# A fused attention and MLP block: one ring of eight raw buffers in the projection, and the MLP's weights staged earlier

## The chip, the cores and the metric

The kernel runs on one core of one Trainium2 chip. The metric is device time in microseconds (us) of one execution, lower is better. Three runs of the kernel before took 1137.27, 1138.0 and 1139.82 us; their median is 1138.0 us.

## The reference

For 2048 tokens of width 448, a gate mixes an attention block of 16 heads (28 wide) and an MLP of inner width 1792. Everything is float32.

```python
qkv = (x @ wqkv) -> q, k, v            # 16 heads of 28
p   = softmax(q @ k.T * 28 ** -0.5)
a   = (p @ v, heads joined) @ wo
y   = layernorm(x)                     # no scale, eps 1e-5
h   = gelu(y @ w1 + b1)                # 448 -> 1792, tanh form
b   = h @ w2 + b2                      # 1792 -> 448
g   = sigmoid((x * gate_w).sum(-1))
out = g * a + (1 - g) * b
```

## The kernel before

**Split operands.** Nearly every float32 operand of a product is split in two: a high part (rounded by ScalarE, ACT, with an `AF.Copy` into the type float32r) and a low part (the raw value minus the high part, a `tensor_sub` on VectorE, DVE, or GpSimd, POOL). A product is then three matmuls on TensorE (PE): high by high, high by low, low by high. So a weight that comes from memory goes through four steps: a DMA into a raw buffer, issued by SyncE (SP), the high part on ACT, the low part on DVE or POOL, and the matmuls. Below, "splitting" a piece means its high and its low part.

**Three stages.** The tokens are worked in four chunks `c` of 512 (`CH`).

1. Projection of q, k, v (`qk_tile`, `v_tile`). For each chunk there are seven tiles `m` of 128 columns of q and k, 11 matmuls each (L179), and then four tiles of 128 tokens of v, 11 matmuls each (L195). A q/k tile is evicted from PSUM by ACT and DVE into one of three `hl` buffers (L181, L182) and stored to `qk` in memory (L183, 512 KB); a v tile goes through one of three `vt` buffers (L197) to `vs` (L199). PSUM has eight banks, and the tiles take them in turn (`next_ps`), so PE may run up to eight tiles ahead of the evictions. The chunk's input is four raw tiles of x (`load_x`, L165 to L170), which are loaded and split while the v tiles of the chunk before are issued. Beside this, chunks 1 and 2 load x a second time for the statistics of the layer norm (`bxr`, L209), and chunks 2 and 3 normalise the MLP's first chunk on POOL and ACT (`ln_apply`, L127 to L133). The raw buffers are two rings here: `wraw`, four buffers for weights, and `xraw`, four for x and the weights of v.
2. MLP (`mlp1`, `mlp2`). For each chunk, 14 tiles `f` of the first layer, 11 matmuls each (L512), into banks 0 and 1 in turn; ACT reads a tile twice (L515, L516: GELU into `hh` and `h`), POOL makes its low part `hl` (L517). Then the second layer for four tiles of 128 tokens, 42 matmuls each (L525, L526, L529). In chunk 0 the weights are still being staged: in each tile `f` the piece `w1[f+3]` and the piece `w2[f]` are fetched, and after `mlp1(c, f)` the pieces `w1[f+2]` and `w2[f-1]` are split (`split_w1`, `split_w2`). The raw buffers for this are four: `s0`, `s1` and the two halves of `lnr`.
3. Attention (`scores`, `pv_mm`), then the output projection.

**The row maxima.** The softmax needs each row's maximum, found from a first, coarse product of q and k: 1024 matmuls of 28 rows (L346), whose results DVE reduces (L326 one bank, L328 two banks). They are spread over the MLP and the attention by a `Filler`: each matmul of the MLP adds its cost to a counter, and when six are due, six row-maximum matmuls into banks 2 to 7 are put between two others. `MLP_MAX` of the 1040 steps (the matmuls and 16 transposes) fall into the MLP, the rest into the attention, three in each pass of its loop. Their keys are in `khr`, loaded in 16 DMAs of 28 rows by 512 (`load_khr`, L408).

**What sets the order.** PE's order is that of the code. In the MLP and the attention the other engines and the SP queue follow the code as well (`tc.manual_schedule`). In the projection a scheduler orders the other engines. All of SP's DMAs go through one queue in order: one that waits for a buffer holds back those behind it.

Of the kernel before, what the change touches and what calls it, by code (L numbers as in the profile page):

```python
# [7 lines left out]
F32 = mybir.dt.float32  # L8
F32R = mybir.dt.float32r
AF = mybir.ActivationFunctionType  # L10
# [30 lines left out]
def kernel(ctx: ExitStack, tc: tile.TileContext, xt, wqk, wv, wo, xk, w1, b1, w2, b2,  # L41
                          ident_d, sel_d, out):
    nc = tc.nc
# [14 lines left out]
    qk = dram.tile([2, 2 * D, S], F32, name="qk")  # L58
# [23 lines left out]
    w1h, w1l, w2h, w2l = {}, {}, {}, {}  # L82
# [10 lines left out]
    def fetch_w1(f):  # L93
        wraw[1, f] = staged()
        nc.sync.dma_start(wraw[1, f], w1[f].rearrange("p t x -> p (t x)"))

    def split_w1(f, lo):
        r = wraw.pop((1, f)).rearrange("p (t x) -> p t x", t=4)
        t = mw1.tile([P, 8, P], F32R, name=f"w1f{f}")
        w1h[f], w1l[f] = t[:, 0:4], t[:, 4:8]  # L100
        nc.scalar.activation(w1h[f], r, AF.Copy)
        lo.tensor_sub(w1l[f], r, w1h[f].bitcast(F32))  # L102

    def fetch_w2(f):
        wraw[2, f] = staged(D)
        nc.sync.dma_start(wraw[2, f], w2[f])

    def split_w2(f):
        r = wraw.pop((2, f))
        nc.scalar.activation(w2h[f], r, AF.Copy)  # L110
        nc.vector.tensor_sub(w2l[f], r, w2h[f].bitcast(F32))

    yh, yl = (my.tile([P, n, CH], F32R, name=f"y{n}") for n in (4, 3))
    lnr = my.tile([P, 2, CH], F32, name="lnr")
# [21 lines left out]
    with tc.tile_pool(name="qx", bufs=2) as qx, tc.tile_pool(name="qo", bufs=3) as qo, \  # L136
# [4 lines left out]
        def next_ps():  # L141
            nonlocal nps
            nps += 1
            return bank[:, nps % 8]

        def load_wqk(m):
            raw = qx.tile([P, 4, P], F32, name="wraw", bufs=4)
            nc.sync.dma_start(raw, wqk[m])
            wh[m] = qw.tile([P, 4, P], F32R, name=f"wh{m}")
            wl[m] = qw.tile([P, 4, P], F32R, name=f"wl{m}")  # L150
            nc.scalar.activation(wh[m], raw, AF.Copy)
            nc.gpsimd.tensor_sub(wl[m], raw, wh[m].bitcast(F32))

        wvh = qw.tile([P, 4, 450], F32R, name="wvh")
        wvl = qw.tile([P, 4, 450], F32R, name="wvl")
        vt = [qw.tile([P, H, 32], F32, name=f"vt{i}") for i in range(3)]

        xh, xl = {}, {}

        def load_x(c, t):  # L160
            if t == 0:
                xh[c] = qx.tile([P, 4, CH], F32R, name="xh")
                xl[c] = qx.tile([P, 3, CH], F32R, name="xl")
            raw = qx.tile([P, CH], F32, name="xraw", bufs=4)
            nc.sync.dma_start(raw, xt[t, :, c * CH:(c + 1) * CH])  # L165
            nc.scalar.activation(xh[c][:, t], raw, AF.Copy)
            if t < 3:
                nc.vector.tensor_sub(xl[c][:, t], raw, xh[c][:, t].bitcast(F32))
            else:
                nc.vector.tensor_sub(xh[c][64:128, t], raw[64:128], xh[c][64:128, t].bitcast(F32))  # L170

        def qk_tile(c, m):
            ps = next_ps()
# [58 lines left out]

        load_wqk(0)
        for t in range(4):
            load_x(0, t)
        load_wqk(1)
        for c in range(NC):
            for m in range(NM):
                if c == 0:
                    if m + 2 < NM:  # L240
                        load_wqk(m + 2)
                    if m == 1:
                        for v in vt:
                            nc.gpsimd.memset(v[:, :, DH:DH + 1], 1.0)
                            nc.gpsimd.memset(v[:, :, DH + 1:32], 0.0)
                    if m == 4:
                        for t in range(4):
                            raw = qx.tile([P, 450], F32, name="xraw", bufs=4)
                            nc.sync.dma_start(raw, wv[:, t])
                            nc.scalar.activation(wvh[:, t], raw, AF.Copy)  # L250
                            nc.gpsimd.tensor_sub(wvl[:, t], raw, wvh[:, t].bitcast(F32))
                qk_tile(c, m)
                if c == 1 and m >= 2 or c == 2 and m < 3:
                    ln_stats(m - 2 if c == 1 else m + 5)
                if c == 1 or c == 2 and m == 0:
# [17 lines left out]
                    ln_rows(TPC, NT)  # L273
                if c == 3 and m == 4:
                    ln_turn(TPC, NT)
                if c == 3 and m in (1, 2, 4):
                    if m == 2:
                        stages += [lnr[:, 0], lnr[:, 1]]
                    fetch_w1(m // 2)
                if c == 3 and m in (4, 5):  # L280
                    split_w1(m - 4, nc.vector)
            for i in range(TPC):
                if c + 1 < NC:
                    load_x(c + 1, i)
                v_tile(c * TPC + i)

    class RowMax:

# [112 lines left out]

    khi = dict.fromkeys(range(MLP_G + 1), khr)

    def load_khr(g, k):

        for j in range(4):
            r = D + (4 * g + j) * DH
            nc.sync.dma_start(khr[32 * j:32 * j + DH, k * CH:(k + 1) * CH].bitcast(F32), qk[0, r:r + DH, k * CH:(k + 1) * CH])  # L408

    def load_khi(g):  # L410
        if g == MLP_G:
# [107 lines left out]
    def mlp2(c, i):  # L519

        sl = slice(i * P, (i + 1) * P)
        last = c * TPC + i == NT - 1
        a = bank[:, 7 if last else i % 2, :D]
        for f in range(NF):
            nc.tensor.matmul(a, hh[f][:, sl], w2h[f], start=(f == 0), stop=False)  # L525
            nc.tensor.matmul(a, hh[f][:, sl], w2l[f], start=False, stop=False)  # L526
            if not last:
                filler.run(2 * W2)
            nc.tensor.matmul(a, hl[f][:, sl], w2h[f], start=False, stop=(f == NF - 1))  # L529
            if not last:  # L530
                filler.run(W2)
            elif f == NF // 3:
# [6 lines left out]
    with tc.manual_schedule(engines={E.SP, E.Pool, E.Activation, E.DVE}):  # L539
        for c in range(NC):  # L540
            for f in range(NF):
                if c == 0:
                    if f + 3 < NF:
                        fetch_w1(f + 3)
                    fetch_w2(f)
                    if f == 0:
                        filler.max = RowMax()
                    if f < 4:
                        load_khr(0, f)
                    if f == FS:  # L550
                        filler.spread(nc.sync, MLP_MAX, 11 * W1 * (0.8 * (NF - FS) + 3 * NF) + 3 * W2 * NF * (NT - 1))
                mlp1(c, f)
                if c == 0:
                    if f + 2 < NF:
                        split_w1(f + 2, nc.vector if f < FS else nc.gpsimd)
                    if f > 0:
                        split_w2(f - 1)
            if c == 0:
                split_w2(NF - 1)
                stages[2:] = []  # L560
            if c == NC - 1:
                m0.close()
# [265 lines left out]
```

## Time and profile before

| what | value |
|---|---|
| median of three runs | 1138.0 us |
| time of the profiled execution | 1136.69 us |
| its span | 1134.9 us |
| PE busy | 1114.4 us, 98% of the span |
| DVE / ACT / POOL busy | 739.6 / 634.6 / 323.8 us |
| mean granted TensorE clock | 0.995 |
| moved by DMA | 84.35 MB |

In this execution the projection runs from 0 to 121 us, the MLP to 474 us and the attention to the end. The "granted clock" is the share of full speed at which TensorE was run. A row of the timeline shows start, duration, engine, line, operation and, in brackets, how long the engine sat idle before and what ended that. Matmul durations overlap, so the distance from one start to the next is what a matmul costs.

### The profile page before, as it was taken

To read this page: it belongs to the slowest core of one execution; us is meant where nothing else is said; L and a number is where in the kernel's file an instruction comes from. 1 tells how busy PE (TensorE), PEld (TensorE's weight loads), DVE (VectorE), ACT (ScalarE), POOL (GpSimd) and SP (SyncE) were. 2 spreads that over 40 slices of the span, in tenths; PEclk is the share of its full clock that TensorE was granted. 3 is DMA by queue.
4 is the path that set the end of the run, shared out by engine and by line. 5 is a ranking of instruction groups with operands and counts; after the bars stand their busy time and mean duration, and the time that the engine had idled before them with its cause. 6 is when DMAs were issued, how large, how long until landed. Compare 5 with 4: busy or idle time off the path is not lost.

```text
span 1134.9 us, 19822 instructions
## 1 busy us (share of the span) xinstructions
PE 1114.4 (98%) x8136; PEld 675.8 (60%) x8136; DVE 739.6 (65%) x1037; ACT 634.6 (56%) x668; POOL 323.8 (29%) x349
## 2 busy tenths in 40 slices
PE   7999999999999999999999999999999999999998
PEld 6878767767767767744444444444444444464556
DVE  3542498888888888576666766667666667646103
ACT  5333660241231132188787877878877788746563
POOL 4005373334333331013113211320223125425050
PEclk9999999999999999999999999999999999999999
DMA  8986642011110105063000220002111003011101
GB/s 264 298 263 230 214 129 72 26 46 35 48 56 25 36 9 129 25 154 99 23 25 19 60 65 24 22 28 51 35 48 36 22 15 93 12 50 51 59 27 50
DMA packets 53519, 84.35 MB, mean 74 GB/s; under 512 B 8676, under 2 KB 28660, under 8 KB 52628
## 3 DMA queue, kind: packets, MB, share of 16 engines
q1 hardware_dynamic: 49236, 76.96, 22.2%
q0 software_dynamic: 4192, 6.12, 2.3%
q8 instruction: 64, 1.05, 0.4%
q14 instruction: 27, 0.22, 0.1%
HBM read 56.40 MB, written 26.49 MB: 73 GB/s over the span
## 4 chain that ended last, share of the span: by engine, by line
PE 90%; DMA 3%; DVE 2%; POOL 2%; issue 1%; ACT 1%; SPq 1%; POOLq 0%; ACTq 0%
PE bank L713 22%; PE bank L466 20%; PE bank L346 15%; PE bank L512 11%; PE bank L179 5%; PE bank L529 4%; PE bank L525 4%; PE bank L526 4%; DMA xraw<-in_xt 2%; PE bank L195 2%; PE bank L618 1%; PE bank L619 1%; PE bank L620 1%; POOL w1f L102 1%; DVE mx L328 1%
## 5 line engine op out<-in xcount | busy, mean ns | idle before, releaser
L471 ACT ACTIVATE pt<-bank 128x1536 f32<-128x1536 f32 (+1 forms) x408 | 482.3, 1234 | 154.0 <-PE bank L466 154.0
L326 DVE TENSOR_REDUCE mx<-bank 128x1 f32<-128x512 f32 x624 | 413.3, 687 | 175.9 <-PE bank L346 162.3
L713 PE MATMUL bank<-pt,vg 128*32 128x512 f32 x2038 | 262.5, 605 | 0.0
L328 DVE TENSOR_REDUCE mx<-bank 128x2 f32<-128x1024 f32 x200 | 235.3, 1218 | 32.3 <-PE bank L346 32.3
L346 PE MATMUL bank<-khi,qd 28*128 28x512 f32 x512 | 241.8, 479 | 1.3 <-DVE mx L326 1.3
L346 PEld LDWEIGHTS bank<-khi,qd 28*128 28x128 f32 x512 | 92.3, 181 | 148.9 <-DVE mx L326 105.4
L466 PE MATMUL bank<-qh,klo 28*128 28x512 f32 x1024 | 177.4, 393 | 0.0
L466 PE MATMUL bank<-qh,khi 29*128 29x512 f32 x768 | 160.0, 481 | 0.0
L512 PE MATMUL bank<-y,w1f 128*128 128x512 f32 x616 | 154.3, 399 | 3.8 <-POOL w1f L102 2.7
L512 PEld LDWEIGHTS bank<-y,w1f 128*128 128x128 f32 x616 | 111.9, 188 | 41.8 <-issue 12.6
L466 PE MATMUL bank<-ql,khi 28*128 28x512 f32 x768 | 132.2, 390 | 0.0
L517 POOL TENSOR_TENSOR hl<-h,hh 128x512 fp32r<-128x512 f32 x56 | 72.4, 1293 | 135.9 <-ACT h L516 93.8
L713 PEld LDWEIGHTS bank<-pt,vg 128*32 128x32 f32 x2038 | 45.6, 108 | 84.1 <-issue 83.5
L515 ACT ACTIVATE hh<-bank,b1s 128x512 fp32r<-128x512 f32 x56 | 38.6, 689 | 99.3 <-PE bank L512 99.2
L466 PEld LDWEIGHTS bank<-qh,klo 28*128 28x128 f32 x1024 | 89.3, 185 | 4.1
L525 PE MATMUL bank<-w2h,hh 128*128 128x448 f32 x224 | 84.0, 375 | 1.8 <-DVE mx L326 1.8
L634 POOL DMA_DIRECT2D lt<-ob x15 | 10.9, 724 | 261.1 <-DVE ob L633 261.1
L529 PE MATMUL bank<-w2h,hl 128*128 128x448 f32 x224 | 85.3, 381 | 0.0
L535 ACT ACTIVATE h<-bank 128x448 f32<-128x448 f32 x16 | 8.7, 546 | 135.4 <-PE bank L529 101.0
L466 PEld LDWEIGHTS bank<-qh,khi 29*128 29x128 f32 x768 | 62.3, 182 | 36.5 <-ACT pt L471 32.2
L526 PE MATMUL bank<-w2l,hh 128*128 128x448 f32 x224 | 82.5, 368 | 0.0
L346 PE MATMUL bank<-khr,qd 28*128 28x512 f32 x512 | 81.0, 466 | 0.2
(112 smaller groups left out, 1241.6 us busy)
## 6 DMA issues: line engine op xcount, KB each, us to landing
qk<-hl SPq DMA_DIRECT2D x28, 512.0 KB
xraw<-in_xt SPq DMA_DIRECT2D x16, 256.0 KB
vs<-vt SPq DMA_DIRECT2D x16, 256.0 KB
s<-in_xt SPq DMA_DIRECT2D x16, 256.0 KB
rc<-rls POOLq DMA_DIRECT2D x60, 64.0 KB, 2.3
bxr<-in_xk SPq DMA_DIRECT2D x8, 448.0 KB
gbs<-h SPq DMA_DIRECT2D x16, 224.0 KB
klo<-qk SPq DMA_DIRECT2D x16, 224.0 KB
```

The costliest lines, as they stand in the source:

```text
L179: nc.tensor.matmul(ps, a, b, start=(i == 0), stop=(i == len(ops) - 1))
L326: nc.vector.reduce_max(self.mx[:, c0:c0 + 1], bank[:, b0], axis=AX)
L328: nc.vector.reduce_max(self.mx[:, c0:c1 + 1:c1 - c0], bank[:, b0:b1 + 1], axis=AX)
L346: nc.tensor.matmul(bank[:, b], self.qds[self.n][r, i * P:(i + 1) * P], khi[self.n // NC][r, k * 512:(k + 1) * 512], start=True, stop=True)
L466: nc.tensor.matmul(bank[:, u % U], a[r, k * P:(k + 1) * P], b[r], start=(i == 0), stop=(i == 2))
L471: nc.scalar.activation(t, bank[:, b:b + len(units)], AF.Exp, scale=SCALE)
L512: nc.tensor.matmul(ps, a, b, start=(i == 0), stop=(i == len(ops) - 1))
L517: nc.gpsimd.tensor_sub(hl[f], h, hh[f].bitcast(F32))
L525: nc.tensor.matmul(a, hh[f][:, sl], w2h[f], start=(f == 0), stop=False)
L526: nc.tensor.matmul(a, hh[f][:, sl], w2l[f], start=False, stop=False)
L529: nc.tensor.matmul(a, hl[f][:, sl], w2h[f], start=False, stop=(f == NF - 1))
L713: nc.tensor.matmul(pv[32 * j:32 * j + 32, :], vg[n // NC][:, k, 32 * j:32 * j + 32], probs.pop(4 * step + j), start=(k == 0), stop=(k == N ...
```

## The change

It has five parts.

1. In the projection the two rings of four raw buffers become one ring of eight (`raw`), which q/k weights, v weights and x share. The v weights are asked for in tile 3 of chunk 0 and not in tile 4. Fetch and split of x are parted: chunk `c+1`'s four raw tiles are fetched at tiles 3 to 6 of chunk `c`, and split after tiles 5 and 6 and ahead of the first two v tiles; before, both stood ahead of the four v tiles.
2. Seven of the 14 pieces of `w1` (before: the splits of two) are fetched into that ring and split during chunk 3 of the projection, their low parts on DVE and POOL in turn.
3. The other seven pieces of `w1` and the 14 of `w2` pass through the four staging buffers in the order `order`, one and a half per tile `f`. A piece's high part is made in one tile and its low part in the tile that follows, ahead of that tile's matmuls. All seven of these low parts of `w1` are POOL's.
4. The row maxima's first keys come in four DMAs of 28 rows by 2048, not 16 of 28 by 512.
5. `MLP_MAX` is 482, not 476. The last but one token tile (`NT - 2`) takes no row-maximum step in its last four `f`, and the attention spreads the rest over two passes fewer.

```diff
-MLP_MAX = 476
+MLP_MAX = 482
...
+        def raw():
+            return qx.tile([P, CH], F32, name="raw", bufs=8)
...
-        def load_x(c, t):
+        def fetch_x(c, t):
+            xraw[c, t] = raw()
+            nc.sync.dma_start(xraw[c, t], xt[t, :, c * CH:(c + 1) * CH])
+
+        def split_x(c, t):
...
+                if c + 1 < NC and m >= 3:
+                    fetch_x(c + 1, m - 3)
                 qk_tile(c, m)
+                if c + 1 < NC and m >= 5:
+                    split_x(c + 1, m - 5)
...
-                if c == 3 and m in (1, 2, 4):
-                    if m == 2:
-                        stages += [lnr[:, 0], lnr[:, 1]]
-                    fetch_w1(m // 2)
-                if c == 3 and m in (4, 5):
-                    split_w1(m - 4, nc.vector)
+                if c == 3:
+                    fetch_w1(m, raw())
+                    if m >= 2:
+                        high_w1(m - 2)
+                        low_w1(m - 2, nc.vector if m % 2 else nc.gpsimd)
             for i in range(TPC):
-                if c + 1 < NC:
-                    load_x(c + 1, i)
+                if c + 1 < NC and i < 2:
+                    split_x(c + 1, i + 2)
                 v_tile(c * TPC + i)
+                if c == 3 and i < 2:
+                    high_w1(i + 5)
+                    low_w1(i + 5, nc.vector if i else nc.gpsimd)
...
+            rows = not last and (c * TPC + i < NT - 2 or f < 10)
...
+        order = [x for i in range(7) for x in (NF + 7 + i, i)] + list(range(7, NF))
...
+            return order[max(0, 3 * (f - 1) // 2 - 1):max(0, 3 * f // 2 - 1)]
...
-                    if f + 3 < NF:
-                        fetch_w1(f + 3)
-                    fetch_w2(f)
                     if f == 0:
+                        stages += [lnr[:, 0], lnr[:, 1]]
                         filler.max = RowMax()
-                    if f < 4:
-                        load_khr(0, f)
+                    for k in stage(f - 1):
+                        low(k)
+                    for k in order[3 * f // 2:3 * (f + 1) // 2]:
+                        fetch_w2(k) if k < NF else fetch_w1(k - NF, staged())
+                    for k in stage(f):
+                        high(k)
+                    if f == 1:
+                        load_khr(0)
...
-    filler.spread(nc.gpsimd, NG * NC * 65, ((NG * NC - 2) * NT + LQ - 1) * 4 // U)
+    filler.spread(nc.gpsimd, NG * NC * 65, ((NG * NC - 2) * NT + LQ - 1) * 4 // U - 2)
```

The SP queue in the projection, from the second half of chunk 1's q/k tiles to its v tiles, before (`xraw<-in_xt` is a raw tile of x for chunk 2, `qk<-hl` a store of a q/k tile, `bxr<-in_xk` x for the statistics, `vs<-vt` a store of a v tile):

```order
L183 DMA qk<-hl 128x2x512 x2
L165 DMA xraw<-in_xt 128x512
L183 DMA qk<-hl 128x2x512
L165 DMA xraw<-in_xt 128x512
L183 DMA qk<-hl 128x2x512
L199 DMA vs<-vt_113 128x512
L165 DMA xraw<-in_xt 128x512
```

and the same stretch of the queue now:

```order
L168 DMA raw<-in_xt 128x512
L218 DMA bxr<-in_xk 128x2x448
L192 DMA qk<-hl 128x2x512 x2
L168 DMA raw<-in_xt 128x512
L192 DMA qk<-hl 128x2x512
L218 DMA bxr<-in_xk 128x2x448
L192 DMA qk<-hl 128x2x512
L208 DMA vs<-vt_113 128x512
```

The last raw tile of x for chunk 2 stood behind the stores of tiles 5 and 6 and the first v store; now it stands ahead of these three.

On ACT, at the start of the MLP (`hh` and `h` are the two GELU reads of a tile `f`, `w1f` and `w2h` the high parts), before:

```order
L515 ACT_TABLE_LOAD
L515 ACTIVATE hh_1063<-bank,b1s 128x512
L516 ACTIVATE h<-bank,b1s 128x512
L101 ACTIVATE w1f_1094<-lnr 128x512
L515 ACTIVATE hh_1061<-bank,b1s 128x512
L516 ACTIVATE h<-bank,b1s 128x512
L101 ACTIVATE w1f_1118<-s_96 128x512
L110 ACTIVATE w2h_1009<-s_97 128x448
```

and now:

```order
L532 ACT_TABLE_LOAD
L532 ACTIVATE hh_1089<-bank,b1s 128x512
L533 ACTIVATE h<-bank,b1s 128x512
L532 ACTIVATE hh_1087<-bank,b1s 128x512
L533 ACTIVATE h<-bank,b1s 128x512
L100 ACTIVATE w1f_1137<-s_97 128x512
L110 ACTIVATE w2h_1035<-lnr 128x448
```

Before, the first `w1f` here is the piece that tile 2 multiplies with; now it is that of tile 7.

On PE, the last two groups of row-maximum steps in the MLP, before (`w2h`, `w2l` with `hh`, `hl` are the second layer; the row behind the `x2` opens the last token tile):

```order
L346 MATMUL bank<-khr,qd 128x512 x6
L529 MATMUL bank<-w2h_1033,hl_1040 128x448
L525 MATMUL bank<-w2h_1035,hh_1037 128x448
L526 MATMUL bank<-w2l_1036,hh_1037 128x448
L529 MATMUL bank<-w2h_1035,hl_1038 128x448
L346 MATMUL bank<-khr,qd 128x512 x2
L525 MATMUL bank<-w2h_1009,hh_1063 128x448
```

and now (the row behind the `x2` is the eleventh `f` of the same token tile, so 12 matmuls stand between it and the last token tile):

```order
L362 MATMUL bank<-khr,qd 128x512 x6
L547 MATMUL bank<-w2h_1051,hl_1074 128x448
L542 MATMUL bank<-w2h_1053,hh_1071 128x448
L543 MATMUL bank<-w2l_1054,hh_1071 128x448
L547 MATMUL bank<-w2h_1053,hl_1072 128x448
L362 MATMUL bank<-khr,qd 128x512 x2
L542 MATMUL bank<-w2h_1055,hh_1069 128x448
```

More of the change, by code (lines that the diff above doesn't have):

```diff
@@ L106, in fetch_w2, with high_w2, low_w2 @@
         nc.sync.dma_start(wraw[2, f], w2[f])
[L108 to L111, printed above, removed]
+    def high_w2(f):
+        nc.scalar.activation(w2h[f], wraw[2, f], AF.Copy)
+    def low_w2(f):
+        nc.vector.tensor_sub(w2l[f], wraw.pop((2, f)), w2h[f].bitcast(F32))
     yh, yl = (my.tile([P, n, CH], F32R, name=f"y{n}") for n in (4, 3))
@@ L539, with high, low, stage @@
     with tc.manual_schedule(engines={E.SP, E.Pool, E.Activation, E.DVE}):
+        order = [x for i in range(7) for x in (NF + 7 + i, i)] + list(range(7, NF))
+        def high(k):
+            high_w2(k) if k < NF else high_w1(k - NF)
+        def low(k):
+            low_w2(k) if k < NF else low_w1(k - NF, nc.gpsimd)
+        def stage(f):
+            return order[max(0, 3 * (f - 1) // 2 - 1):max(0, 3 * f // 2 - 1)]
         for c in range(NC):
```

69 lines of the change are left out of this document (35 added, 34 removed).

## The prediction

> **What bounds the kernel now.** I read the page first: who is busy, and where the slices of the span are not full.
>
> ```profile
> PE 1114.4 (98%) x8136; PEld 675.8 (60%) x8136; DVE 739.6 (65%) x1037; ACT 634.6 (56%) x668; POOL 323.8 (29%) x349
> ```
>
> TensorE is the bound; what can be gained without taking matmuls away is its idle time and the matmuls that run at a lower clock. Next, who PE waits for (us in total, times, longest):
>
> ```profile
> PE bank L179 <- ACT xh L166: 6.1, 1, 6.1
> PE bank L512 <- POOL w1f L102: 2.7, 5, 1.0
> PE bank L179 <- DVE xh L170: 2.4, 1, 2.4
> PE bank L525 <- DVE mx L326: 1.8, 1, 1.8
> PE bank L512 <- DVE w1f L102: 1.0, 2, 0.7
> ```
>
> The first is the start of the program, whose first five DMAs the change leaves as they are. The other four are the change's aims. Then stretches around the two longest of them (busy time of each engine, and behind POOL the granted clock, the DMA share and GB/s):
>
> ```profile
> 64.20:67.10 2.90, 0.47 (x2) 0.03 (x1) 0.71 (x2) 1.40 (x3) 0.00 (x0) 1.00 0.85 309
> 68.60:72.00 3.40, 3.40 (x9) 2.67 (x8) 1.45 (x6) 0.79 (x2) 0.00 (x0) 0.51 0.82 108
> 471.30:474.00 2.70, 2.70 (x9) 2.34 (x8) 0.00 (x0) 0.00 (x0) 0.00 (x0) 0.50 0.00 0
> ```
>
> A wait costs twice: shortly after PE resumes, the clock is at half for some 3 us (0.51 and 0.50).
>
> **The change part by part.** All sums are against the profiled execution: span 1134.9, time 1136.7, which is 1.3 us under the median of the three runs and 0.6 under the lowest.
>
> *x for chunk 2.* PE's timeline, with the first two matmuls of the chunk and the first at full clock again:
>
> ```profile
> 62.05 0.40 PE L179 MATMUL bank<-xh,wh 128*128 128x512 f32 x1
> 62.28 0.40 PE L179 MATMUL bank<-xl,wh 128*128 128x512 f32 x1
> ...
> 72.00 0.40 PE L179 MATMUL bank<-xh,wh 128*128 128x512 f32 x1
> ```
>
> Between 62.05 and 72.00 run two tiles: 22 matmuls at 0.23 us (62.05 to 62.28) and two short transposes make 5.2 us; 9.95 passed. So 4.7 us are lost, wait and half clock together. The fourth raw tile of x was issued late, behind stores:
>
> ```profile
> 56.72 0.36 SPq L183 DMA_DIRECT2D qk<-hl  x1
> 58.09 0.39 SPq L183 DMA_DIRECT2D qk<-hl  x1
> 59.55 0.33 SPq L199 DMA_DIRECT2D vs<-vt  x1
> 59.94 1.17 SPq L165 DMA_DIRECT2D xraw<-in_xt  x1
> ```
>
> It now stands ahead of two stores of 512 KB and one of 256, which is 1.28 MB or about 4 us at the 309 GB/s above. It was needed 2.4 us sooner than it came, so the wait goes: **-4.7**.
>
> *The first weights.* Chunk 0's and chunk 1's first layers (x154 matmuls; the next number but one is first to last start):
>
> ```profile
> L512 PE MATMUL bank<-y,w1f x154: 387/389/504, 121.0 to 167.4; 128*128 128x512 f32 x154
> L512 PE MATMUL bank<-y,w1f x154: 387/389/501, 211.3 to 256.0; 128*128 128x512 f32 x154
> 215.84 0.73 PE L346 MATMUL bank<-khr,qd 28*128 28x512 f32 x6
> 216.50 3.49 PE L512 MATMUL bank<-y,w1f 128*128 128x512 f32 x14
> 219.92 0.73 PE L346 MATMUL bank<-khr,qd 28*128 28x512 f32 x6
> ```
>
> One group of six row-maximum steps and 14 matmuls take 4.08 us (215.84 to 219.92); 14 at 0.23 are 3.2, so a group costs about 0.86. Chunk 1 has 12 groups in its 44.7 us, chunk 0 has six: without waits it would take 44.7 - 5.2 = 39.5. It takes 46.4; the two estimates of a matmul, 0.23 and slightly less, leave an excess of 6.3 to 6.9, say 6.6 us. The reason is that each piece of `w1` is ready just in time, behind POOL's work on the tile before:
>
> ```profile
> 154.01 0.73 PE L512 MATMUL bank<-y,w1f 128*128 128x512 f32 x2 [0.99 <-POOL w1f L102]
> 151.44 1.30 POOL L517 TENSOR_TENSOR hl<-h,hh 128x512 fp32r<-128x512 f32 x1 [1.87 <-ACT h L516]
> 152.69 1.27 POOL L102 TENSOR_TENSOR w1f<-lnr,w1f 128x512 fp32r<-128x512 f32 x1
> ```
>
> Now pieces 0 to 6 lie ready when the MLP starts, and piece `f` from 7 on is complete two to four tiles ahead. What is late next is ACT: a high part that waits for its DMA holds back the GELU reads behind it, and with two banks PE stands two tiles later. The closest is the piece for tile 9: its buffer is freed by POOL behind `hl` of tile 2 (1.30 + 1.27 us), the DMA takes about 3.1 (99.47 to 102.53 below), and ACT wants it one tile later. I leave 0.7 us for that (0 to 3.3, half of the excess): **-5.9**.
>
> *A new wait at tile 2.* Tile 2 needs bank 0 back from the first GELU reads. ACT before:
>
> ```profile
> 99.47 0.33 SPq L95 DMA_DIRECT2D s<-in_w  x1
> 102.53 0.63 ACT L101 ACTIVATE w1f<-s 128x512 fp32r<-128x512 f32 x1 [3.59 <-DMA s<-in_w]
> 103.06 0.62 ACT L129 ACTIVATE y<-s 128x512 fp32r<-128x512 f32 x1
> 110.19 0.60 ACT L181 ACTIVATE hl<-bank 128x512 fp32r<-128x512 f32 x1 [3.80 <-DMA qk<-hl]
> 122.52 0.55 ACT L197 ACTIVATE vt<-bank 128x448 f32<-128x448 f32 x1 [3.05 <-DMA vs<-vt]
> 124.96 0.68 ACT L516 ACTIVATE h<-bank,b1s 128x512 f32<-128x512 f32 x1
> ```
>
> In chunk 3 ACT does not follow PE: its evictions stand behind the layer norm's `y` (103.06), then wait for stores to free `hl` and `vt`, and the reads of tile 0 end at 125.6. PE will be 4.7 us earlier, so it starts the MLP at 116.3 and wants bank 0 two tiles (5.1 us) later, at 121.4. If ACT's chain doesn't move, PE waits 4.2 us; if it moves by as much as PE, nothing. The chain begins at the load of `lnr`, behind the x tiles and stores of chunk 2, which leave when the v tiles of chunk 1 are evicted, no longer stuck behind the late x: I take half of 4.7, so a wait of 1.9. The half clock followed idle gaps of 1.8 and 2.4 us, and not one of 0.99; 3.4 and 2.7 us at half speed (the stretches above) cost 1.7 and 1.3, on average 1.5, of which I take half. **+2.6** (0 to 5.7). By the Trainium skill (TensorE: Matmul & The Clock Gate, Part 1: The HAM clock gate) the clock falls after an idle window of about 3.4 us. By that rule this term is 1.9 alone; the trace differs, with half clock after 2.4 and 1.8 us.
>
> *The end of the staging.* Four low parts of `w2` instead of two now stand on DVE right ahead of the row maxima of the second layer's first groups:
>
> ```profile
> 170.39 0.61 DVE L111 TENSOR_TENSOR w2l<-lnr,w2h 128x448 fp32r<-128x448 f32 x1
> 174.39 1.09 PE L346 MATMUL bank<-khr,qd 28*128 28x512 f32 x6
> ```
>
> Two more are 1.2 us, and the group at 174.39 already waits for DVE (1.09 against the 0.73 at 215.84). **+1.0** (0 to 1.5).
>
> *The end of the MLP.*
>
> ```profile
> 467.46 0.50 PE L346 MATMUL bank<-khr,qd 28*128 28x512 f32 x2
> 469.79 0.47 PE L525 MATMUL bank<-w2h,hh 128*128 128x448 f32 x1 [1.82 <-DVE mx L326]
> 470.10 0.36 PE L526 MATMUL bank<-w2l,hh 128*128 128x448 f32 x1
> 470.30 0.37 PE L529 MATMUL bank<-w2h,hl 128*128 128x448 f32 x1
> ...
> 471.32 0.58 PE L526 MATMUL bank<-w2l,hh 128*128 128x448 f32 x1
> 471.69 0.58 PE L529 MATMUL bank<-w2h,hl 128*128 128x448 f32 x1
> ```
>
> The last token tile uses bank 7, which DVE still reduces: 2.3 us from 467.46 to 469.79, of which 0.3 would pass anyway. Now 12 matmuls of 0.20 us (470.10 to 470.30), 2.4 us, stand in between, so the reductions are done in time. From 471.3 a matmul takes 0.37; eight of them at 0.17 over are 1.3. **-3.3** (-2.5 if 0.8 of the wait stays).
>
> *Six more row-maximum steps in the MLP* are one more group, **+0.9**. In the attention six fewer, a group of six takes 0.73 us by itself (215.84), so at most 0.7, and I take **-0.2**, since other matmuls run beside them
> *Taken at nothing*: the fetch of the last q/k weights and of the v weights in chunk 0 (PE has no wait there after the start; a low part of POOL that came late would cost up to its 1.3 us), and the keys in four DMAs. The first of these waits for a store of chunk 3, and the v stores behind it could be held back; the stores in front of them are later than that anyway. If not, it adds to the wait at tile 2, inside its bounds.
>
> **Sum**: -4.7 - 5.9 + 2.6 + 1.0 - 3.3 + 0.9 - 0.2 = -9.6, so 1127.1 against 1136.7. The timed runs lie 0.6 to 3.1 over the profiled one; adding 0.9, I forecast 1128.0.
>
> **The rivals.**
>
> *All covers hold*: ACT's chain moves as far as PE, no wait at tile 2 or behind the staging, none in it: 2.6 + 1.0 + 0.7 less, 1123.7. For it: the chain's first link is the stores that the late x held up. Against it: the stores' waits (3.80, 3.05) are the memory's pace, and more weights are loaded there.
>
> *What chunk 2 gains, tile 2 gives back*: ACT's chain stays, PE waits 4.2 us and pays a full half-clock phase, 3.1 more than the forecast: 1131.1; with half of the staging excess kept, 1133.7. For it: POOL's layer norm stands on a load of its own, and has a low part of `w1` more in front of it.
>
> *x still comes late*: the earlier fetch is eaten by a full memory (the DMA share was 0.85 there), and PE's wait stays; then the wait at tile 2 is gone too, 1128.0 + 4.7 - 2.6 = 1130.1.
>
> *The staging loop becomes the bound* (slower): 21 pieces pass through four buffers, 5.25 rounds each. A round is a DMA (3.1), a high part (0.63) in ACT's turn, POOL's `hl` and the low part (2.6), one tile later by rule. Without waits the stage takes 46.4 - 6.6 = 39.8 us, which allows 7.6 us a round. At 10 us it takes 52.5, which is 6.1 over the old stage in place of 5.9 under it: 1128.0 + 12.0 = 1140.0. From there on the change is slower. Against it: before, 26 pieces went through four buffers in 46.4 us, 7.1 us a round, and that with each piece in demand at once. For it: high and low part now stand a tile apart.
>
> **How the numbers follow.** 0.2% of 1138.0 is 2.3 us, about what a measurement of this kernel tells from no change: faster is below 1135.7, slower above 1140.3. Chances: the forecast 0.50, all covers 0.15, tile 2 gives back 0.15, x still late 0.06, the staging loop 0.14, of which 0.09 above 1140.3 and 0.05 between. That makes 0.86 faster, 0.05 the same, 0.09 slower. The range goes from 1122.5, just under the case of all covers, to 1135.5, over the two rivals in the middle with the unknown ends of the other terms; it leaves out the staging loop and a little below.
>
> **What would show it.** Right: no wait for `xh` near 62 us and the granted clock at 1.00 there; the MLP's first matmul near 116 us; the first layer of chunk 0 no longer than 43 us; no wait for `w1f`; at the MLP's end no wait for `mx` and no half clock. The new wait would stand at tile 2, ended by ACT `h`. Wrong: a wait over 5 us at tile 2, evictions that stop PE in chunk 3, or tiles of chunk 0 that stand behind ACT all along.

## The result, and the profile after

The changed kernel takes 1139.83 us (median of 14 runs), the kernel before 1138.49 us (14 runs, 1136.72 to 1139.82). Twelve runs of the changed kernel lie at 1138.3 to 1140.7 us, the two others at 1133.67 and 1130.73. The ratio on record is 1.0002 (the quotient of the two medians is 1.0012), with a 95% interval of 0.9987 to 1.0017: no difference that can be told, where 1128.0 us was forecast with a range up to 1135.5. The profiled execution of the changed kernel takes 1140.1 us with a span of 1138.32, which is 3.4 us over the span before (1134.89). The stages lie so (us; a stage ends where PE starts the next one's first matmul):

| stage | before | after | difference | forecast |
|---|---|---|---|---|
| projection | 120.99 | 117.25 | -3.7 | -4.7 |
| MLP chunk 0, first layer | 46.7 | 49.0 | +2.3 | -3.3 |
| MLP chunk 0, second layer | 43.6 | 47.8 | +4.2 | +1.9 |
| MLP, chunk 1 to chunk 3's first layer | 223.3 | 223.5 | +0.2 | 0 |
| chunk 3, second layer | 39.8 | 37.1 | -2.7 | -3.3 |
| attention, to PE's end | 656.8 | 654.2 | -2.6 | -0.2 |
| from PE's end to the end of the span | 3.7 | 9.4 | +5.7 | 0 |

The windows of the changed kernel at the places of the prediction (busy time of PE, PEld, DVE, ACT and POOL, the granted clock, the DMA share, GB/s), the first two and the sixth being the old waits:

```profile
64.00:67.00 3.00, 3.00 (x16) 2.34 (x15) 1.41 (x6) 0.50 (x1) 0.00 (x0) 1.00 0.95 277
68.60:72.00 3.40, 3.40 (x17) 2.78 (x16) 2.67 (x10) 1.31 (x3) 0.00 (x0) 1.00 1.00 296
122.35:128.59 6.24, 0.08 (x1) 0.00 (x1) 0.16 (x1) 3.14 (x5) 0.00 (x0) 0.71 0.97 342
128.60:132.70 4.10, 4.10 (x11) 3.25 (x12) 0.85 (x1) 2.08 (x4) 2.52 (x2) 0.61 0.50 108
176.10:179.50 3.40, 3.40 (x11) 2.99 (x11) 1.82 (x2) 0.00 (x0) 2.55 (x2) 0.51 0.01 5
471.60:474.40 2.80, 2.80 (x15) 2.61 (x14) 0.00 (x0) 0.55 (x1) 0.00 (x0) 1.00 0.22 82
1132.00:1137.50 5.50, 0.00 (x0) 0.00 (x0) 0.00 (x0) 0.00 (x0) 0.00 (x0) 0.50 0.00 0
```

The waits aimed at are gone, with full clock at 64 to 72 us and at 472. In their place stand a hole of 6.2 us at tile 2 with a half-clock stretch behind it, another half-clock stretch at 176, and 5.5 us at the very end in which no engine is busy and no DMA moves. Who PE waits for says the same of the first:

```profile
PE bank L529 <- ACT h L533: 6.4, 2, 6.2
PE bank L188 <- ACT xh L175: 5.8, 1, 5.8
PE bank L362 <- DVE mx L344: 1.5, 4, 0.6
```

(L188, L529, L362 are now the matmuls of the q/k tiles, of the MLP's first layer and of the row maxima.) The hole at the end is in no list of waits, since nothing computes after it. It shows in the line at which the program ends: counts, then minimum, median and maximum in ns. Before and after:

```profile
L823 POOLq DRAIN  x3: 40/102/1412, 1128.9 to 1134.6; - x3
```

```profile
L856 POOLq DRAIN  x3: 40/102/10967, 1126.6 to 1138.1; - x3
```

POOL's last subtraction begins at 1126.6 us (1128.9 before), and its last drain is recorded from there: 10.97 us in place of 1.41. The records with which the other engines end stand behind it, at 1137.7 us. The drain is 9.6 us longer and the stretch behind PE's end only 5.7, since before, SP's last stores (issued from 1130.13 us on) ended later than POOL.

### The profile page after: what moved, and what is told of

The parts are those of the page before. It is cut to its first block, busy times and chain, and to the rows that moved or that the text cites. A ratio compares the mean times of both kernels' runs of the same rounds, so it can differ in the third digit from the quotient of the medians.

```text
span 1138.3 us, 19785 instructions
## 1 busy us (share of the span) xinstructions
PE 1114.2 (98%) x8136; PEld 678.9 (60%) x8136; DVE 739.6 (65%) x1031; ACT 633.9 (56%) x668; POOL 327.2 (29%) x348
## 3 DMA queue, kind: packets, MB, share of 16 engines
q0 software_dynamic: 4064, 5.89, 2.2%
## 4 chain that ended last, share of the span: by engine, by line
PE 94%; DMA 2%; DVE 1%; ACT 1%; issue 0%; SPq 0%; POOL 0%; ACTq 0%; DVEq 0%
PE bank L746 22%; PE bank L483 21%; PE bank L362 15%; PE bank L529 12%; PE bank L188 6%; PE bank L547 4%; PE bank L542 4%; PE bank L543 4%; PE bank L204 2%; PE bank L651 1%; PE bank L652 1%; PE bank L653 1%; DMA qk<-hl 1%; DMA raw<-in_xt 0%; DVE mx L344 0%
## 5 line engine op out<-in xcount | busy, mean ns | idle before, releaser
L344 DVE TENSOR_REDUCE mx<-bank 128x2 f32<-128x1024 f32 x203 | 238.8, 1219 | 32.5 <-PE bank L362 32.5
L362 PE MATMUL bank<-khi,qd 28*128 28x512 f32 x512 | 240.7, 479 | 0.1
L362 PEld LDWEIGHTS bank<-khi,qd 28*128 28x128 f32 x512 | 92.3, 181 | 148.1 <-DVE mx L342 105.0
L529 PE MATMUL bank<-y,w1f 128*128 128x512 f32 x616 | 154.1, 401 | 6.4 <-ACT h L533 6.4
L529 PEld LDWEIGHTS bank<-y,w1f 128*128 128x128 f32 x616 | 113.5, 190 | 42.1 <-issue 12.3
L362 PE MATMUL bank<-khr,qd 28*128 28x512 f32 x512 | 79.8, 466 | 1.5 <-DVE mx L344 1.5
```

Of the source, the lines that this page charges most:

```text
L344: nc.vector.reduce_max(self.mx[:, c0:c1 + 1:c1 - c0], bank[:, b0:b1 + 1], axis=AX)
L362: nc.tensor.matmul(bank[:, b], self.qds[self.n][r, i * P:(i + 1) * P], khi[self.n // NC][r, k * 512:(k + 1) * 512], start=True, stop=True)
L529: nc.tensor.matmul(ps, a, b, start=(i == 0), stop=(i == len(ops) - 1))
```

## The experiments

Three losses had to be explained: the tail, the wait at tile 2, and the second layer of chunk 0. The edits are against the changed kernel if not said otherwise.

### The tail: how many DMAs POOL has issued

With `MLP_MAX` at 482 the last load of `qd` before the attention, four DMAs, falls into the MLP, where SP issues it. POOL issues 127 DMAs (4064 packets in its queue) and not 131 (4192). To give it four others:

```diff
-        nc.sync.dma_start(worw[g], wo[:, g])
+        nc.gpsimd.dma_start(worw[g], wo[:, g])
```

> The changed kernel with the four loads of wo issued by POOL in place of SP, early in the attention. POOL then issues 131 DMAs, as the kernel before does, in place of 127; nothing else is changed. Theory D (the length of POOL's last instruction, the drain at the end of the program, hangs on how many DMAs POOL has issued, counted round a queue of 128: 131 leaves 3, and 1.41 us were measured; 127 leaves 127, and 10.97 us were measured): the drain is under 2.5 us, the span ends about 1 us behind SP's last store, and the time falls by about 6, from 1139.8 to 1133 to 1134. Rival D2 (the drain's length has to do with when POOL comes to its end, or with chance, not with the count): the drain stays at 9 to 12 us and the time at 1139 to 1141.

Measured: 1133.05 us (six runs), ratio to the kernel before 0.9948 [0.9929, 0.9967]. The drain is short:

```profile
L856 POOLq DRAIN  x3: 46/102/1406, 1125.5 to 1131.4; - x3
```

The opposite, in the kernel before:

```diff
-MLP_MAX = 476
+MLP_MAX = 482
```

> The kernel before with the row maxima's share in the MLP raised from 476 to 482 steps, nothing else. A load of four DMAs then falls into the MLP, where SP issues it, and POOL issues 127 DMAs and not 131. Theory D (by the count): the drain at the end is 10 to 12 us in place of 1.41, and the time rises by 5 to 8 us, to 1143 to 1146. Rival D2 (by the time of the end or by chance): a drain of 1 to 2 us, and a time within 1 us of the kernel before (six steps more in the MLP +0.9, six fewer in the attention -0.2 to -2).

Measured: 1145.2 us (four runs), 1.0063 [1.0047, 1.0078], with the drain at

```profile
L823 POOLq DRAIN  x3: 46/102/10965, 1134.1 to 1145.5; - x3
```

So one number, with no other part of the change, makes the drain long and the kernel 7 us slower. In the profile, the slowest of the four runs, the stretch behind PE's end is 9.4 us, 5.7 over the kernel before; the rest of what it lost lies ahead of PE's end. Four other counts follow. The row maxima's loads and stores of the attention given to SP leave 90 DMAs:

```diff
-    filler.spread(nc.gpsimd, NG * NC * 65, ...)
+    filler.spread(nc.sync, NG * NC * 65, ...)
```

> The changed kernel with the row maxima's loads and stores in the attention issued by SP and not by POOL; POOL issues only the 90 DMAs that belong to the softmax's sums. A look at the drain alone; the time may also change since SP's queue gets 37 DMAs more. Theory D in its linear form (some 0.075 us for each DMA past a turn of 128, over 1.2): about 8 us. If the drain is rather a matter of yes or no (short once the queue has turned round, else long): about 11 us. Rival D2: anything, without relation to the count.

With the q loads of all passes but the first issued by POOL, 247:

```diff
-                nc.sync.dma_start(qs[n][i]...
+                (nc.gpsimd if n else nc.sync).dma_start(qs[n][i]...
```

> The changed kernel with the q loads of the attention (15 times 8) issued by POOL, which then issues 247 DMAs. A look at the drain alone. If its length goes by the count round 128 (247 leaves 119, and 0.082 us each were the difference of 127 and 90): 10 to 10.6 us. If it is only long as long as the queue has never turned round: about 1.4 us. If it goes by the whole count: about 20 us.

With those of passes 1 to 5 (`if 0 < n < 6`), 167:

> The changed kernel with the q loads of five of the 16 passes of the attention (5 times 8) issued by POOL, which then issues 167 DMAs, 39 past a turn of 128. A look at the drain. By the straight line through 3 (1.41) and 127 (10.97): 4.2 us. By the line through 90 (7.94) and 127: 3.8. If the drain is short for any count some way past 128 and long only close below a full turn: under 2 us.

And with a single one of the `wo` loads (`nc.sync if g else nc.gpsimd`), 128, in the version of all three single changes, below:

> The version with all three single changes, with one of the four loads of wo issued by POOL and three by SP, so that POOL issues 128 DMAs, one full turn if a turn is 128. A look at the drain: 1.2 to 1.4 us if a full turn leaves nothing, 11 us if it leaves 128.

| DMAs issued by POOL | past a turn of 128 | drain, us |
|---|---|---|
| 131 (seven kernels) | 3 | 1.40 to 1.41 |
| 167 | 39 | 4.35 |
| 90 | 90 | 7.94 |
| 247 | 119 | 10.88 |
| 127 (five kernels) | 127 | 10.96 to 10.97 |
| 128 | 128 | 11.04 |

```profile
L856 POOLq DRAIN  x3: 40/102/4349, 1125.3 to 1131.1; - x3
```

The row is that of 167. The order holds with no exception, and 247 speaks against the whole count as well as against "short once it has gone round". The line is not quite straight: by the one through 3 and 127, 119 would take 10.35, half a microsecond less than it did. A full turn costs as much as any. What POOL does in that time the trace doesn't tell. A drain costs only what stands out behind the last stores: with 167 DMAs, from PE's end to the end of the span, it is 3.7 us, as in the kernel before. By the Trainium skill (VectorE: DVE Perf Modes, The DRAIN you can't avoid) the drains of the frame around a program take about 12 ns each. SP's take 7 ns here; POOL's last takes 1.4 to 11 us, and no run shows whether it is one of those that the section means.

### The wait at tile 2: a subtraction near 17 us

The kernel with 90 POOL DMAs differs from the changed kernel in the attention only, and yet waited 1.9 us at tile 2 and not 6.2. So the same instructions end in two ways. The two runs part in chunk 0 of the projection. DVE, POOL and SP in the changed kernel (L177 a low part of x for chunk 1, L191 the eviction of a q/k tile, L261 and L157 low parts of weights, L192 the store of a q/k tile):

```profile
17.57 4.62 DVE L177 TENSOR_TENSOR xl<-raw,xh 128x512 fp32r<-128x512 f32 x1 [1.10 <-ACT xh L175]
22.11 0.68 DVE L191 TENSOR_TENSOR hl<-bank,hl 128x512 fp32r<-128x512 f32 x1
...
9.90 6.35 POOL L157 TENSOR_TENSOR wl<-raw,wh 128x512 fp32r<-128x512 f32 x5 [4.50 <-DMA raw<-in_wqk]
16.20 4.17 POOL L261 TENSOR_TENSOR wvl<-raw,wvh 128x450 fp32r<-128x450 f32 x4
20.32 1.31 POOL L157 TENSOR_TENSOR wl<-raw,wh 128x512 fp32r<-128x512 f32 x1
```

```profile
16.96 0.52 SPq L168 DMA_DIRECT2D raw<-in_xt  x1
22.82 0.38 SPq L192 DMA_DIRECT2D qk<-hl  x1
```

and in the run with the short wait:

```profile
17.03 1.17 DVE L177 TENSOR_TENSOR xl<-raw,xh 128x512 fp32r<-128x512 f32 x1 [1.24 <-ACT xh L175]
...
16.29 0.49 SPq L168 DMA_DIRECT2D raw<-in_xt  x1
18.89 0.38 SPq L192 DMA_DIRECT2D qk<-hl  x1
```

The subtraction takes 0.69 us elsewhere. Here it ends 0.6 us after POOL has come to the end of ten low parts made without a pause (20.32 + 1.31); in all seven profiles in which it took over 4 us, it ended 0.5 to 0.6 us after that run of POOL's. The eviction stands behind it on DVE, the store behind the eviction, and SP's queue behind the store: 5.3 us without an issue (17.5 to 22.8). The DMA share (last column but one) of the stretch from 20 to 23 us, in the changed kernel and in the other run:

```profile
20.00:23.00 3.00, 3.00 (x14) 2.44 (x13) 3.00 (x3) 1.43 (x3) 1.64 (x2) 1.00 0.39 148
```

```profile
20.00:23.00 3.00, 3.00 (x15) 2.46 (x14) 1.60 (x3) 1.84 (x4) 1.43 (x2) 1.00 0.84 277
```

From 45 us on ACT's instructions come 3.0 to 5.9 us earlier in the other run, up to the first GELU read:

```profile
127.27 0.69 ACT L532 ACTIVATE hh<-bank,b1s 128x512 fp32r<-128x512 f32 x1
```

```profile
122.28 0.69 ACT L532 ACTIVATE hh<-bank,b1s 128x512 fp32r<-128x512 f32 x1
```

PE, eight banks ahead, sees nothing of it for 100 us. By the Trainium skill (SBUF — State Buffer, Who interferes with whom) a DVE instruction with two inputs in SBUF contends with a GpSimd instruction that reads SBUF, and the ports that they share are "an exclusive lock". The trace agrees with the contention and goes further: POOL's instructions took 1.04 to 1.3 us each here, and the loser lost some four in a row. The evictions (L191, one input in PSUM) kept their 0.68.

The test takes the two subtractions away from DVE:

```diff
-                nc.vector.tensor_sub(xl[c][:, t], r, ...)
+                (nc.gpsimd if c == 1 and t < 2 else nc.vector).tensor_sub(xl[c][:, t], r, ...)
```

> The changed kernel with the low parts of the first two raw x tiles of chunk 1 made by POOL, in its own turn, and not by DVE. Theory C (a chain that begins at 17.6 us: the first of these subtractions, two operands in SBUF on DVE, stands for 4.62 us in place of 0.69 while POOL makes ten low parts without a pause; the eviction behind it, the store of that tile and with it SP's queue stand too, the chain of stores, x and evictions runs 4 to 5 us late from there to the MLP, and PE pays at tile 2): DVE's evictions near 18 to 23 us take 0.7 us each, SP does not stand from 17.5 to 22.8, ACT's first GELU reads come 3 to 5 us earlier (near 123), the wait at tile 2 falls from 6.2 to 1 to 3 us; time 1133 to 1136, with the drain at the end still at 11 us. Rival (the delay is the memory's pace and only shifts; the run with the short wait was chance): the wait at tile 2 stays over 4.5 us, and the time at 1138 to 1140.

Measured: 1132.18 us (six runs), 0.9951 [0.9935, 0.9966]. SP no longer stands from 17.5 to 22.8 us (it issues at 19.62 and 20.09), and the first GELU read comes at 124.04. The wait at tile 2 in the profile is 3.8 us, over what theory C allowed, and the time is under it. In the profiles with that edit the wait was 3.8, 0.4, 1.6 and, with 16 key DMAs, nothing. With the subtractions on DVE and the key DMAs as in the change it was 6.2, 5.9, 5.4 and 6.2 where the first took over 4 us, and 1.9, 0.9 and 1.3 where it took under 1.4. The profiles with the long subtraction (5.4 to 6.2 us) don't overlap with the others (0 to 3.8), so the subtraction is the larger part of the cause; what makes up the rest, up to 3.8 us, is not shown. Nor is what decides whether the subtraction is long: it began at 16.9 to 18.2 us where it was, and at 17.0 to 17.7 where it was not.

### The keys in four DMAs

The other place at which SP stands is just ahead of the last stores of the projection. The changed kernel, SP and a stretch of windows:

```profile
114.85 0.69 SPq L240 DMA_DIRECT2D lns<-rows  x1
119.03 0.32 SPq L425 DMA_DIRECT2D khr<-qk  x1
119.44 1.41 SPq L192 DMA_DIRECT2D qk<-hl  x2
120.94 1.67 SPq L208 DMA_DIRECT2D vs<-vt  x2
```

```profile
117.70:120.70 3.00, 3.00 (x15) 2.46 (x14) 1.13 (x4) 1.58 (x4) 0.00 (x0) 1.00 0.29 83
```

A key DMA over all 2048 columns needs the last chunk's tile 3 in memory; it waits for that store at the head of the queue, two q/k stores and the v stores stand behind it, and the memory is at 0.29 from 117.7 us on. From 115.5 to 117.7, the first 2.2 us of its wait, the DMA share is full, at 407 GB/s, so that not all of this wait is lost. In 16 DMAs:

```diff
-                    if f == 1:
-                        load_khr(0)
+                    if f < 4:
+                        load_khr(0, f)
```

> The changed kernel with part 4 undone: the row maxima's first keys in 16 DMAs of 28 rows by 512 over tiles 0 to 3 of the MLP. Theory K (the first of the four long key DMAs needs the last chunk's tile 3 in memory, waits for it at the head of SP's queue from 115.5 to 119.0 us while the memory runs empty, and the last stores of the projection stand behind it): the gap on SP near 115 to 119 goes, the last GELU reads come 3 to 4 us earlier, PE's wait at tile 2 of the MLP falls from 6.3 to 2 to 3.5 us, the time by 3 to 4.5 us, to 1135 to 1137, if the end stays as it is. Rival S (the stores' and weight loads' pace through the memory sets ACT's chain; something else would wait in its place): the wait at tile 2 stays over 5 us and the time within 1 us of the changed kernel's. Both leave the drain at the end at 11 us by theory D, since POOL issues 127 DMAs.

Measured: 1133.66 us (11 runs), 0.9959 [0.9943, 0.9975]. In its profile, at 1139.81 us the slowest of its runs, the wait at tile 2 is 4.3 us: 1.9 less, where 3 to 4 were expected. The median is lower by more than the forecast, and clear of the intervals, but the timed runs also hold the chance of the subtraction. So the keys were tried twice more in the version that has the short drain and the low parts of `w2` on POOL, but DVE's subtraction as it was (below), once in 16 DMAs and once in four, at tile 3:

> The version without the x low parts on POOL (131 DMAs, the last three w2 low parts on POOL; 1128.9 us, 0.9914 of the kernel before), with the first keys in 16 DMAs as in the kernel before. Theory K (the first long key DMA holds SP's queue for 3 us ahead of the projection's last stores, which costs once the chain is late): in runs with the long subtraction on DVE the wait at tile 2 is 4 us in place of 6, the median falls by 2 to 3 us, ratio 0.988 to 0.990. Rival (the keys only change places with other waits): ratio 0.990 to 0.993.

> The same version with the four long key DMAs at tile 3 and not at tile 1 of the MLP, behind all stores of the projection. Theory K: what costs is the place in SP's queue and not the number of DMAs, so the gap near 115 to 119 us goes, the last GELU-ready eviction comes 3 us earlier, and the median falls by 2 to 4 us, ratio 0.987 to 0.990. If the length of the DMAs matters and not their place, or neither: 0.990 to 0.993.

With 16: 1126.9 us (six runs), 0.9900 [0.9882, 0.9917], against 0.9914 [0.9894, 0.9934] without that edit. The profile has the long subtraction (4.87 us) and a wait of 3.0 us. Later in the queue: 1136.68 us (12 runs), 0.9990 [0.9980, 1.0000]; theory K failed on the time. The wait at tile 2 is 3.4 us, also with the long subtraction (4.63 us), but the keys came too late:

```profile
PE bank L362 <- DMA khr<-qk: 3.6, 3, 2.0
PE bank L529 <- ACT h L533: 3.4, 1, 3.4
```

```profile
122.97 0.32 SPq L208 DMA_DIRECT2D vs<-vt  x1
134.59 0.34 SPq L95 DMA_DIRECT2D s<-in_w  x1
135.02 0.38 SPq L107 DMA_DIRECT2D lnr<-in_w  x1
135.45 0.83 SPq L425 DMA_DIRECT2D khr<-qk  x2
```

They stood behind a weight load that waits for a staging buffer until 134.6, and the first row maxima waited for them. So where the subtraction is long, the place in the queue does move the wait at tile 2 (2 to 3 us), and keys that come later cost more than that elsewhere. What 16 DMAs are worth in time stays open: as the only edit they took 0.43% off the ratio (about 5 us), and in the versions with other edits 0.12 to 0.14%, which their intervals don't tell from nothing. How often the subtraction was long in the timed runs is not known.

### The second layer of chunk 0: low parts ahead of the row maxima

The groups of row maxima there, in the changed kernel:

```profile
172.52 0.50 PE L362 MATMUL bank<-khr,qd 28*128 28x512 f32 x2
173.45 0.50 PE L362 MATMUL bank<-khr,qd 28*128 28x512 f32 x2 [0.43 <-DVE mx L344]
174.58 0.50 PE L362 MATMUL bank<-khr,qd 28*128 28x512 f32 x2 [0.64 <-DVE mx L344]
```

The six take 2.5 us (172.52 to 175.0) in place of 0.7, and half clock follows at 176.1. Three of the four low parts of `w2` on DVE ahead of them go to POOL:

```diff
-    def low_w2(f):
-        nc.vector.tensor_sub(w2l[f], ...)
+    def low_w2(f, lo=nc.vector):
+        lo.tensor_sub(w2l[f], ...)
...
                     high(k)
-                    low(k)
+                    low_w2(k, nc.gpsimd)
```

> The changed kernel with the last three low parts of w2 made by POOL and not by DVE. Theory W (four low parts of w2 in a row on DVE hold back the row maxima, whose group at 172.5 us then takes 2.5 us in place of 0.73 and is followed by half clock in some runs): that group takes about 0.8 us, no half clock near 176, and the second layer of chunk 0 takes 44.5 to 45.5 us in place of 47.8 (46.2 where the half clock stayed out); time 2 to 3 us less, 1136 to 1138. Rival (DVE is behind by then anyway, by the reductions alone): under 0.7 us are gained.

Measured: 1134.24 us (five runs), 0.9961 [0.9944, 0.9977], more than expected; its profile is one with the short subtraction. The second layer of chunk 0 (first to last start of the first of its three matmuls) is what the edit touches. Changed kernel, then this one:

```profile
L542 PE MATMUL bank<-w2h,hh x56: 361/366/575, 166.2 to 213.4; 128*128 128x448 f32 x56
```

```profile
L542 PE MATMUL bank<-w2h,hh x56: 361/365/477, 161.0 to 205.0; 128*128 128x448 f32 x56
```

47.2 us against 44.0, as theory W has it; the group, at 171.83 us there, takes 0.73 us, and the clock is at 1.00 from 170 to 185. In all the seven profiles with this edit the stage took 44.6 to 44.7 us to the next chunk, in the seven others of this layout 46.2 to 47.8. In three of these, at 47.8, half clock followed the group; in three others (131, 247 and 167 DMAs) nearly the same gaps (0.5 and 0.6 us) brought none, and the stage took 46.2 to 46.3.

### All three

> The changed kernel with three of the single changes together: the first two x low parts of chunk 1 on POOL, the last three w2 low parts on POOL, and the four loads of wo issued by POOL, so that POOL issues 131 DMAs. If the three losses are independent (tail 9.6, chain 3 to 4.5, second layer 2 to 3 of the profiled runs): 1139.8 less 9.6 less 3.7 less 2.5 plus about 2.3 for the part of the tail that SP's last store covers, 1125 to 1128, which is the time that was forecast for the change. If they hide one another: 1130 or more.

Measured: 1123.36 us (five runs, 1121.5 to 1126.8), 0.9882 [0.9865, 0.9899], under the range that the sum gave. The wait at tile 2 is 0.4 us, the mean granted clock 1.000. Part of the surplus does not come from the three losses: from the second layer's last matmul to PE's end, where these edits change nothing but who issues the loads of `wo`, this profile takes 645.4 us and that of the changed kernel 647.2. In all eight profiles with the edit of the subtractions or of the low parts of `w2` it is 645.3 to 645.5 us, in the three with neither and the same q loads 647.0 to 647.2 (131, 127 and 90 DMAs). The reason is not known. With the keys in 16 DMAs as well:

> The version with all three single changes (the first two x low parts of chunk 1 and the last three w2 low parts on POOL, 131 DMAs of POOL), and the first keys in 16 DMAs as in the kernel before. Theory K (the long key DMA holds SP's queue for 3 us ahead of the last stores): with the chain early the wait at tile 2 was 0.4 us in the one profile and more in slower runs, so 0 to 2 us less than with four key DMAs, a ratio to the kernel before of 0.986 to 0.988 where that one had 0.988. Rival (with the chain early the keys lie beside other work): a ratio within 0.001 of 0.988, or over it, since 12 more DMAs are issued by SP.

1122.94 us (four runs), 0.9870 [0.9851, 0.9889]: the same within the intervals, as the rival had it. Without the edit of the subtractions:

> The version with all three single changes, without that of the x low parts: DVE makes them again. Theory C: in most runs, as in the profiles of the changed kernel, of the one with 131 DMAs, of the one with 16 key DMAs and of the one with q loads on POOL, the first subtraction near 17 us stands for over 4 us, and the tile-2 wait is 4 to 6 us; in some it is 1.2 us. The timed runs fall in two groups some 5 us apart, with the median 3 to 5 us over the version with x low parts on POOL: 1127 to 1129, a ratio to the kernel before of 0.991 to 0.993 against 0.988. Rival (the wait has to do with memory, not with POOL and DVE): the same ratio as there, 0.988.

1128.92 us (six runs), 0.9914 [0.9894, 0.9934]: one run at 1123.06, whose profile has the short subtraction (1.37 us), and five at 1128.2 to 1130.6. That is the two groups that theory C asked for, some 6 us apart. The five have no profile, so that their subtraction was the long one is not shown; their granted clock is 0.996 to 0.998, and 1.000 in the one at 1123.06 us.

## Why the prediction was wrong

It named the waits that go, and they went. It failed by three steps, and two smaller ones went against each other. One of its own signs of being wrong came, a wait over 5 us at tile 2.

- **The end of the program had no step at all.** The prediction counted PE's time and what is moved between queues for what it does there and then. "Six more row-maximum steps" was priced as matmuls only; that four DMAs change queues with them was not followed. +5.7 us in the span. With the tail mended, the changed kernel takes 1133.05.
- **A new wait at tile 2: +2.6 forecast, with 5.7 as its upper end.** PE lost 7.9 us from tile 1's start to tile 3's (119.77 to 132.71, less 5.0 for two tiles): a wait of 6.2 and a half-clock stretch. The step assumed that ACT's chain moves with PE's or stays. In this profile it came later than before (first GELU read at 127.27, 124.37 before); in the profile with the short subtraction and the same edits up to here it came earlier, at 122.28. The premise, that the chain begins at the load of `lnr`, was wrong: it begins at 17 us, since x is fetched and split earlier now and one subtraction meets POOL's ten low parts. In the kernel before, the first two of them came when POOL was nearly through (21.5 us), and lost 0.7 us:

```profile
20.58 2.08 DVE L168 TENSOR_TENSOR xl<-xraw,xh 128x512 fp32r<-128x512 f32 x2 [1.65 <-ACT xh L166]
```

  The rival that foresaw a give-back at tile 2 (1131.1 to 1133.7) is near to what the kernel does without its tail; that is the number alone, since ACT's chain did not stay but came later.
- **Keys in four DMAs, "taken at nothing".** They were said to stand behind stores that are later anyway. The long DMA stood ahead of six stores, waited for 3.4 us, and accounts for some 2 to 3 us of the wait at tile 2 where the subtraction is long.
- **The end of the staging and six more steps: +1.9 forecast, +4.2 measured.** The mechanism was right (DVE late for the group behind four low parts), the size was not: the group took 1.8 us more than a free one, and half clock followed it (0.51 from 176.1 to 179.5), which the bounds of 0 to 1.5 left out. The rule of the Trainium skill that the prediction weighed (TensorE: Matmul & The Clock Gate, Part 1: The HAM clock gate; an idle window of about 3.4 us) doesn't cover this one: the longest gap just ahead of it was 0.64 us.
- **x for chunk 2 (-4.7) and the end of the MLP (-3.3)** were right: no wait, full clock. The two tiles of chunk 2 take 5.3 us (63.16 to 68.47) in place of 9.95, which is 4.6 less, and the MLP's end 2.7 less. The projection gained only 3.7, mainly because its first two tiles took 8.8 us (5.79 to 14.55) in place of 7.3: matmuls started 0.43 us apart or more up to 12.2 us, before up to 10.4. In the other profiles these two tiles took 7.2 to 9.4 us, so this is no effect of the change that can be told.
- **The first weights (-5.9).** Right: tiles 3 to 13 take 33.5 us (132.71 to 166.22) in place of 37.8, and 1.3 us of excess in tiles 0 to 2 before is inside the loss at tile 2 now. The staging loop, the slower rival, did not become the bound.
- **The attention (-0.2)** gained 2.6 us. "Two passes fewer" was read as six steps. In the kernel before, the last two steps of the row maxima (1046.88 and 1048.32) and the transpose of their result stand almost alone on PE, which waits for DVE twice (0.95 and 1.04 us) and then runs at a lower clock:

```profile
1046.90:1050.00 3.10, 1.11 (x4) 0.42 (x3) 2.19 (x4) 0.00 (x0) 3.00 (x3) 1.00 0.20 74
1050.00:1055.00 5.00, 5.00 (x32) 1.69 (x31) 0.28 (x1) 2.37 (x2) 0.85 (x2) 0.66 0.03 7
```

The change spreads the steps over fewer passes, so that the last one comes at 1041.13 us; PE then waits 0.58 us for DVE, and no stretch of the attention shows a lower clock up to PE's end. The kernel before with 482 steps, which has six fewer in the attention but as many passes as before, keeps both waits and the lower clock (0.85 from 1050 to 1060 us), so it is the passes that gained and not the six steps.

The forecast sum of -9.6 and these corrections (tail +5.7, tile 2 +5.3, second layer +2.3, projection +1.0, MLP's end +0.6, weights +0.3, attention -2.4) give +3.2 for the span; +3.4 was measured. What half clock follows a gap, and which way the subtraction at 17 us falls in a given run, stays open.

## What to carry to other kernels

A change that moves a few instructions to another queue or another engine is to be followed to the end of the program and not only to the next wait: here four DMAs less on one queue cost about 6 us, as much as the largest gain. Where an engine runs far ahead of a chain that feeds it much later, the delay is made where the chain stands first; compare the start times of two runs instruction by instruction and look for the first that differs. And where DVE's work with both inputs in SBUF falls beside a long unbroken run of POOL's, price it at the end of that run.

## What was not expected of the hardware

- POOL's last drain grew with the number of DMAs that it had issued past a turn of 128: 1.41 us at 131, 4.35 at 167, 7.94 at 90, 10.97 at 127, 11.04 at 128.
- A subtraction of 0.69 us with both inputs in SBUF stood for 4.3 to 5.0 us on DVE while POOL made low parts without a pause, in 7 of the 10 profiles in which it met them; in the three others 1.17 to 1.37.
